# A halt in GpSimd's load queue, and a new order of the first two head pairs, in a fused attention and feed-forward kernel

## The chip, the cores and the metric

The kernel runs on one core of one Trainium2 chip. The metric is the device time of one execution in microseconds (us), as the median of the runs. TensorE is called PE in the profile (PEld for its weight loads), VectorE DVE, ScalarE ACT, GpSimd POOL and SyncE SP. A time in the trace counts from the start of the profiled span.

## What is computed

The reference is attention with a relative position bias, and behind it two matrix products with a leaky ReLU between them. Cut to what matters:

```python
B, H, S, D = 8, 8, 576, 64
scores = q @ k.T / sqrt(D) + bias_table[bucket(i - j)]   # per batch and head, 576 x 576
attn   = softmax(scores)
x      = (attn @ v)  # heads side by side: 4608 tokens x 512
h      = x @ w_in    # 512 x 2048
out    = max(0.01 * h, h) @ w_out                          # 2048 x 512
```

## The kernel before, in words

Work is tiled by head pairs: 8 batches of 4 pairs, 32 items, and n is the number of the item. A pair's q and k are turned on PE into `qt` and `kt` (`transpose_q`, `transpose_k`, lines 290 to 302); ACT copies q out of PSUM in the first pairs (line 293), DVE copies k (line 300) and masks its tail (`apart`, line 285). `kt` has two buffers, so the k of pair n overwrites that of pair n-2.

`score(n, u)` (line 823) makes one part of the scores on PE and their exponential on ACT. There are six parts: u = 0 to 3 give 128 keys each against 512 queries of both heads (PE line 322, ACT line 335, 128x1024), u = 4 the last 64 queries (PE line 315, ACT line 338 twice), u = 5 the last 64 keys (PE lines 325 and 326, ACT line 342). PSUM holds two score tiles for u = 0 to 3 and 5, so PE's third score waits for ACT to have read the first. Below, "s03" is short for score(0, 3), and so on.

The bias is applied after the exponential, as a product: `band(n, u)` (line 358, DVE) multiplies the part of the weights near the diagonal with a table `hk` (or `hk4` for the last 64 keys). The table is built at the start: ACT and DVE make one row of 512 numbers for each head, SP writes it to DRAM (line 189) and reads it back shifted for each partition (`load_hk`, `load_hk4`, lines 190 to 208) in the order: heads 0 and 1 of `hk`, pair 0 of `hk4` (two loads), heads 2 and 3 of `hk`, the other pairs of `hk4` (two loads), heads 4 to 7 of `hk`.

Then `av_tails(n)` and `av(n, e)` (PE lines 371 and 382) multiply the weights with v for the two heads, DVE divides (`divide`, lines 391 and 393), and `x_transposes` (PE line 443, DVE line 444) turns the pair's output into `xT`, from which the feed-forward pieces are made: `ffn_in` (PE line 469), `leaky` (ACT line 482 mostly), `ffn_out` (PE line 510).

All five engines have an order written out by hand (`manual_schedule`): each runs its instructions in the order of the calls. q, k, v and the weights are loaded, with a cast to bf16, by DMAs that GpSimd issues one after another. Each of GpSimd's loads also waits, by a semaphore that it shares, for the load eight before it. Their order at the start (lines 154 and 218 to 230, then `loads(0)`, line 782) is: q and k of heads 0 and 1; of 2 and 3; of 4 and 5; v of head 0; v of head 1; the two halves of the v tails of batch 0 (`load_v_tail`, line 130); v of head 2; v of head 3; q and k of heads 6 and 7; q and k of batch 1, heads 0 to 3; v of heads 4 to 7 in four parts (line 119); the ones columns of batch 1's v (two memsets); q and k of batch 1, heads 4 to 7; the first half of `w_in`; v of batch 1 in four parts and its tails; the second half of `w_in`; and `w_out`.

The first four pairs run in the loop of lines 832 to 870, with no feed-forward work beside them as no `xT` is complete. In it the order for n = 0 on PE is: s02, k of pair 1, three dummy matmuls (`spin(3)`, line 774), s03, q of pair 1, three dummy matmuls, s05, s04, s10, s11. For n = 1: the bands of pair 0 (DVE), k of pair 2, three dummy matmuls, s12, `av_tails(0)`, `av(0, 0)`, `band(1, 0)`, s13, q of pair 2, `av(0, 1)`, s15, `band(1, 1)`, s20, `x_transposes(0)`, `band(1, 2)`, s14, s21. From n = 4 on feed-forward pieces stand between the parts of a pair.

`tick` (line 780) is a tile of one element. GpSimd copies one element of an earlier pair's output into it (line 796) ahead of a group of later loads, so these are issued only after that pair.

Of the kernel before, what the change touches and what calls it, by code (L numbers as in the profile page):

```python
# [11 lines left out]
BF16 = mybir.dt.bfloat16  # L12
# [25 lines left out]
def kernel(  # L38
# [10 lines left out]
    nc = tc.nc  # L49

    B, H, S, D = q.shape
# [4 lines left out]
    P = 128  # L56
    n_pairs = H // 2
    NJ = S // P
    SL = S - NJ * P
# [10 lines left out]
    per = ctx.enter_context(tc.tile_pool(name="per", bufs=1))  # L70
# [20 lines left out]
    hk = per.tile([P, H, 3 * P], BF16, name="hk")  # L91
    hk4 = per.tile([P, n_pairs, P + SL], BF16, name="hk4")

    NBUF = 2
# [5 lines left out]
    v4 = [per.tile([P, n_pairs, D + 1], BF16, name=f"v4_{i}") for i in range(NBUF)]  # L100
# [8 lines left out]
    def load_qk(b, h0, h1):  # L109
        i = b % NBUF  # L110
        for src, dst in ((q, qn[i]), (k, kn[i])):
            nc.gpsimd.dma_start(  # L112
                out=dst[0:RQ, h0:h1, :, :].rearrange("r h c d -> r h (c d)"),
                in_=src[b, h0:h1, :, :].rearrange("h (r c) d -> r h (c d)", c=NC),
            )
# [8 lines left out]
    def load_v_head(b, h):  # L124
        nc.gpsimd.dma_start(  # L125
            out=vn[b % NBUF][:, :, h, 0:D],
            in_=v[b, h, 0 : NJ * P, :].rearrange("(c s) d -> s c d", s=P),
        )

    def load_v_tail(b):  # L130
        for e in range(2):
            nc.gpsimd.dma_start(
                out=v4[b % NBUF][e * SL : (e + 1) * SL, :, 0:D],
                in_=v[b, e::2, NJ * P : S, :].rearrange("h s d -> s h d"),
            )

    def clear_v(eng, i):
# [40 lines left out]
    for j, (u, lo, w, m) in enumerate(groups):  # L178
        copy = nc.scalar.copy if j % 3 == 2 else nc.vector.tensor_copy
        copy(out=ub[:, C0 + lo : C0 + lo + m * w].rearrange("h (m w) -> h m w", w=w),  # L180
             in_=e8[:, u : u + m].unsqueeze(2).to_broadcast([H, m, w]))
    row = ub[:, :]
    nc.vector.tensor_copy(
        out=ub[:, C0 - BAND + 1 : C0],
        in_=bass.AP(tensor=row.tensor, offset=row.offset + C0 + BAND - 1,
                    ap=[list(row.ap[0]), [-1, BAND - 1]]),
# [23 lines left out]
    def mirrored(t, lo, hi):  # L210
# [4 lines left out]
        ap[-1][0] = -1  # L215
        return bass.AP(tensor=v.tensor, offset=v.offset + hi - lo - 1, ap=ap)

    load_qk(0, 2, 4)
    load_qk(0, 4, 6)
    clear_edges(nc.vector, 1)  # L220
    load_v_head(0, 0)
    load_v_head(0, 1)
    load_v_tail(0)
    load_v_head(0, 2)
    load_v_head(0, 3)
    load_qk(0, 6, H)
# [39 lines left out]
    def turned_pair(n, j):  # L266

        if by_dma(n):
            return turned[n][:, j * NC : (j + 1) * NC, :].rearrange("p c r -> p r c")
        ps = ps_m_pool.tile([P, 8 * P], BF16, name="ps_t", tag="m")  # L270
        b, p = items[n]
        for c in range(NC):
            if n > n_pairs + 1:
                nc.tensor.transpose(ps[:, c * RQ : (c + 1) * RQ], in_=prs[n][:, j, c, :],
                                    identity=ident[0:RQ, 0:RQ])
                continue
            for e in range(2):
                nc.tensor.transpose(ps[e * D : (e + 1) * D, c * RQ : (c + 1) * RQ],
                                    in_=(qn, kn)[j][b % NBUF][0:RQ, 2 * p + e, c, :],
                                    identity=ident[0:RQ, 0:RQ])  # L280
        return ps[:, 0:S].rearrange("p (c r) -> p r c", c=NC)

    def apart(t):

        nc.vector.tensor_tensor(
            out=t[:, S : S + P].rearrange("p (e i) -> p e i", e=2),
            in0=t[:, NJ * P : S].unsqueeze(1).to_broadcast([P, 2, SL]),
            in1=own, op=ALU.mult)

    def transpose_q(n):  # L290
        qt = qts[n] = qt_pool.tile([P, S], BF16, name="qt")
        copy = nc.scalar.copy if n <= n_pairs else nc.vector.tensor_copy
        copy(out=qt[:, 0:S].rearrange("p (r c) -> p r c", c=NC), in_=turned_pair(n, 0))

    def transpose_k(n):
        kt = kts[n] = kts_[n % 2]
        t = turned_pair(n, 1)
        cuts = [0, -(-P // NC), RQ] if n == 0 else [0, RQ]
        for lo, hi in zip(cuts, cuts[1:]):
            nc.vector.tensor_copy(out=kt[:, lo * NC : hi * NC].rearrange("p (r c) -> p r c", c=NC),  # L300
                                  in_=t[:, lo:hi, :])
        apart(kt)
# [41 lines left out]
    def band(n, u):  # L344
        b, p = items[n]
        at, at4 = at_view(n), at4_[n % 2]
        hp = hk[:, 2 * p : 2 * p + 2, :]
        if u == 0:
            o, m = at[:, :, 0, 0 : 2 * P], mirrored(hp, P, 3 * P)
        elif u in (1, 2):  # L350
            o, m = at[:, :, u, (u - 1) * P : (u + 2) * P], mirrored(hp, 0, 3 * P)
        elif u == NJ:
            o, m = at[:, :, 3, 2 * P : S], mirrored(hp, 0, S - 2 * P)
        elif u == NJ + 1:
            o, m = at4[:, 3 * P : S], mirrored(hk4[:, p, :], 0, P + SL)
        else:
            return
        nc.vector.tensor_tensor(out=o, in0=o, in1=m, op=ALU.mult)  # L358
# [3 lines left out]
    def av_tails(n):  # L362

        b, p = items[n]
        at4 = at4_[n % 2]
        ops_[n] = op_pool.tile([P, NJ + 1, 2 * D], BF16, name="opair")
        ps = outs[n] = [ps_o_pool.tile([P, 512], FP32, name="ps_o", tag=f"o{e}") for e in range(2)]
        for ic in range(NJ + 1):
            for e in range(2):
                r = slice(e * SL, (e + 1) * SL)  # L370
                nc.tensor.matmul(ps[e][:, ic * (D + 1) : (ic + 1) * (D + 1)],  # L371
                                 lhsT=at4[r, ic * P : (ic + 1) * P], rhs=v4[b % NBUF][r, p, :],
                                 start=(ic == 0), stop=False)

    def av(n, e):
        b, p = items[n]
        at = at_[n % 2]
        ps = outs[n][e][:, 0 : (NJ + 1) * (D + 1)].rearrange("p (i d) -> p i d", d=D + 1)
        for ic in range(NJ + 1):
            for c in range(NJ):  # L380
                o = (e * NJ + c) * S + ic * P
                nc.tensor.matmul(ps[:, ic, :], lhsT=at[:, o : o + P], rhs=vn[b % NBUF][:, c, 2 * p + e, :],  # L382
                                 start=False, stop=(ic == NJ and c == NJ - 1))
        divide(n, (e,))
# [40 lines left out]
    def x_by_dma(n):  # L425
        return n_pairs + 2 <= n < N - 1 and n != 2 * n_pairs - 1

    def x_transposes(n, spare=None):
        b, p = items[n]
        opair = ops_[n]  # L430
        w = (NJ + 1) * P
        if x_by_dma(n):
            nc.sync.dma_start_transpose(
                out=xT[p][:, b * S : b * S + w].rearrange("p (i t) -> p i t", t=P),
                in_=opair.rearrange("p i d -> p (i d)"),
            )
            return
        if spare is None:
            ps = ps_m_pool.tile([P, 8 * P], BF16, name="ps_tx", tag="m")
        else:  # L440
            ps = ps_o_pool.tile([P, 8 * P], BF16, name="ps_tx", tag=spare)
        for ic in range(NJ + 1):
            nc.tensor.transpose(ps[:, ic * P : (ic + 1) * P], in_=opair[:, ic, :], identity=ident)  # L443
        nc.vector.tensor_copy(out=xT[p][:, b * S : (b + 1) * S], in_=ps[:, 0:S])
# [326 lines left out]
    def spin(k):  # L771
        pw = ps_o_pool.tile([P, 512], FP32, name="ps_w", tag="o0")
        for _ in range(k):
            nc.tensor.matmul(pw, lhsT=ones[:, 0:P], rhs=ones, start=True, stop=True)
# [2 lines left out]
        for u in range(NJ + 2):  # L777
            band(n, u)

    tick = per.tile([1, 1], BF16, name="tick")  # L780

    def loads(n, behind_pair=2):

        b, p = items[n]
# [22 lines left out]
    def begin(n):  # L807
        loads(n)
        if by_dma(n + 1):
            turn_ahead(n)  # L810
# [12 lines left out]
    def score(n, u):  # L823
        exp(n, u, qk_mm(n, u))
# [4 lines left out]
    spin(2)  # L829
    score(0, 0)  # L830
    score(0, 1)
    for n in range(n_pairs):
        begin(n)
        if n > 1:
            band(n - 1, 5)
            band(n - 1, 4)
        if n == 1:
            for u in (0, 1, 2, 5, 4):
                band(0, u)
        if n == 0:  # L840
            score(n, 2)
        transpose_k(n + 1)
        if n < 2:
            spin(3)
        if n > 0:
            score(n, 2)
            av_tails(n - 1)
            av(n - 1, 0)
            band(n, 0)
        score(n, 3)  # L850
        if n == 1:
            transpose_q(n + 1)
        if n > 0:
            av(n - 1, 1)
        if n != 1:
            transpose_q(n + 1)
        if n < 1:
            spin(3)
        score(n, 5)
        if n > 0:  # L860
            band(n, 1)
        if n == 1:
            score(n + 1, 0)
        if n > 0:
            x_transposes(n - 1)
            band(n, 2)
        score(n, 4)
        if n != 1:
            score(n + 1, 0)
        score(n + 1, 1)  # L870

    n = n_pairs
# [141 lines left out]
```

## Time and profile before

| | before |
|---|---|
| median of 3 runs | 370.7 us |
| range of the runs | 370.27 to 371.1 us |
| profiled execution, its own time | 370.79 us |
| profiled execution, its span | 369.0 us |
| PE busy in the span | 360.6 us (98%) |
| ACT busy in the span | 245.7 us (67%) |
| DVE busy in the span | 192.9 us (52%) |

The span reaches from the first to the last instruction of the program; the 1.8 us between it and the execution's own time lie around it. A timeline row gives the start, the time to the end of the last instruction of the row, the engine, line, operation and operands, how many instructions are merged, and in brackets the idle time of the engine before the row and what ended it. DMA queue q0 is that of the loads that GpSimd issues, q1 that of SP's.

### The profile page before, as it was taken

Reading aid. Unit: us, or ns where it says so; the run is one execution under the profiler, and the core shown is the slowest. Engines: PE = TensorE matmul, PEld = TensorE weight load, DVE = VectorE, ACT = ScalarE, POOL = GpSimd, SP = SyncE. Lnnn points to the kernel's source line nnn. Section 1 sums busy time; section 2 is a strip of 40 time slices with the busy share of each in tenths; the row PEclk is TensorE's granted clock in tenths of the full one; section 3 lists DMA queues with packets and bytes.
Section 4 is the critical chain, followed back from the end, with each engine's and each line's share of the span. In section 5 each row is a group of like instructions: output and inputs, shape, how many; then the busy total and the mean of one; then the engine's idle time right before and its main releaser. Section 6 shows DMA issues by size and latency. Waiting matters only on the chain.

```text
span 369.0 us, 10548 instructions
## 1 busy us (share of the span) xinstructions
PE 360.6 (98%) x4496; PEld 188.1 (51%) x4496; DVE 192.9 (52%) x502; ACT 245.7 (67%) x382; POOL 75.4 (20%) x118
## 2 busy tenths in 40 slices
PE   7989999999999999999999999999999999999996
PEld 2555555555555555555555545455555544444443
DVE  4688687776757576766765556665554200200000
ACT  5998887479847797777877777777777365055111
POOL 8853431063006300630053006100000000000000
PEclk9999999999999999999999999999999999999999
DMA  8999999969937992899099558933111000110212
GB/s 107 191 197 183 206 203 141 160 114 154 136 80 126 172 155 53 120 157 197 20 134 183 115 80 97 174 98 72 28 47 50 28 30 0 69 47 0 76 69 85
DMA packets 104358, 40.17 MB, mean 109 GB/s; under 512 B 83184, under 2 KB 98808, under 8 KB 104312
## 3 DMA queue, kind: packets, MB, share of 16 engines
q0 software_dynamic: 53696, 18.36, 49.3%
q1 hardware_dynamic: 49320, 19.06, 29.2%
q10 hardware_dynamic: 1296, 2.10, 1.6%
q8 instruction: 35, 0.57, 0.6%
q14 instruction: 11, 0.09, 0.1%
HBM read 37.68 MB, written 9.45 MB: 128 GB/s over the span
## 4 chain that ended last, share of the span: by engine, by line
PE 91%; DMA 4%; POOL 2%; DVE 1%; ACT 1%; issue 1%; ACTq 0%; POOLq 0%
PE pm L469 30%; PE pm L510 28%; PE pm L629 9%; PE ps_s L322 7%; PE ps_o L417 6%; DMA vn<-in_v_dram 4%; PE ps_o L382 4%; PE ps_s L325 2%; PE ps_o L371 1%; PE ps_q L315 1%; PE pm L503 1%; PE ps_tx L443 1%; POOL vn L125 1%; POOL kn L112 1%; POOL qn L112 0%
## 5 line engine op out<-in xcount | busy, mean ns | idle before, releaser
L335 ACT ACTIVATE at<-ps_s 128x1024 bf16<-128x1024 f32 x128 | 124.8, 1026 | 25.2 <-PE ps_s L322 24.9
L482 ACT ACTIVATE gt<-pm 128x512 bf16<-128x512 f32 x138 | 83.2, 603 | 69.4 <-PE pm L469 68.8
L469 PE MATMUL pm<-xT,w_in_sb 128*128 128x512 bf16 x508 | 117.2, 379 | 0.1
L510 PE MATMUL pm<-w_out_sb,gt 128*128 128x512 bf16 x476 | 110.5, 380 | 0.0
L358 DVE TENSOR_TENSOR at<-at,hk 128x768 bf16<-128x768 bf16 (+3 forms) x160 | 70.7, 453 | 55.5 <-ACT at L335 31.3
L469 PEld LDWEIGHTS <-w_in_sb 128*128 128x128 bf16 x508 | 47.9, 98 | 55.2
L510 PEld LDWEIGHTS <-gt 128*128 128x128 bf16 x476 | 43.4, 98 | 49.6
L322 PE MATMUL ps_s<-qt,kt 64*128 64x512 bf16 x256 | 43.4, 380 | 2.2 <-ACT at L335 1.6
L629 PE MATMUL pm<-w_out_sb,gt 64*128 64x512 bf16 x168 | 42.0, 376 | 0.0
L523 DVE COPY y<-pm 128x512 f32<-128x512 f32 x28 | 19.4, 691 | 41.4 <-PE pm L510 41.4
L629 PE MATMUL pm<-xT,w_in_sb 64*128 64x512 bf16 x136 | 37.5, 376 | 0.0
L393 DVE TENSOR_TENSOR opair<-ps_o,rcp 128x320 bf16<-128x320 f32 x64 | 29.7, 488 | 1.4
L796 POOL COPY tick<-opair 1x1 bf16<-1x1 bf16 x18 | 3.2, 180 | 130.7 <-DVE opair L393 130.7
L119 POOL DMA_DIRECT2D vn<-in_v_dram x32 | 28.0, 887 | 8.8 <-DMA w_out_sb<-in_moe_w_out_dram 4.6
L417 PE MATMUL ps_o<-vn,at 64*128 64x65 bf16 x1520 | 29.5, 190 | 0.0
L417 PEld LDWEIGHTS <-at 64*128 64x128 bf16 x1520 | 27.1, 94 | 4.4 <-SPq L401 3.0
L322 PEld LDWEIGHTS <-kt 64*128 64x128 bf16 x256 | 11.5, 94 | 22.5 <-issue 13.3
L342 ACT ACTIVATE at<-ps_s 128x576 bf16<-128x576 f32 x32 | 21.8, 682 | 0.2 <-PE ps_s L326 0.2
L338 ACT ACTIVATE at<-ps_q 128x256 bf16<-128x256 f32 x64 | 21.3, 395 | 0.4 <-PE ps_q L315 0.3
L391 DVE RECIPROCAL rcp<-ps_o 128x5 f32<-128x5 f32 x64 | 10.0, 181 | 21.1 <-PE ps_o L382 18.0
L382 PE MATMUL ps_o<-vn,at 128*128 128x65 bf16 x520 | 20.4, 194 | 0.1
L382 PEld LDWEIGHTS <-at 128*128 128x128 bf16 x520 | 17.9, 97 | 3.3 <-issue 0.9
(65 smaller groups left out, 257.4 us busy)
## 6 DMA issues: line engine op xcount, KB each, us to landing
out_dram<-y SPq DMA_DIRECT2D x28, 256.0 KB, 2.5
qn<-in_q_dram POOLq DMA_DIRECT2D x14, 288.0 KB, 7.3
kn<-in_k_dram POOLq DMA_DIRECT2D x14, 288.0 KB, 9.2
vn<-in_v_dram POOLq DMA_DIRECT2D x28, 128.0 KB, 9.7
w_in_sb<-in_moe_w_in_dram POOLq DMA_DIRECT2D x2, 1024.0 KB, 12.9
w_out_sb<-in_moe_w_out_dram POOLq DMA_DIRECT2D x2, 1024.0 KB, 15.9
out_dram<-y ACTq DMA_DIRECT2D x7, 256.0 KB, 2.0
qn<-in_q_dram POOLq DMA_DIRECT2D x4, 144.0 KB, 3.8
```

The source lines that it names most:

```text
L119: nc.gpsimd.dma_start(out=vn[b % NBUF][:, c, h0:h1, 0:D], in_=v[b, h0:h1, c * P : (c + 1) * P, :].rearrange("h s d -> s h d"),)
L322: nc.tensor.matmul(ps[:, e, :], lhsT=kt[r, u * P : (u + 1) * P], rhs=qt[r, 0:512], start=True, stop=True)
L335: nc.scalar.activation(at[:, :, u, 0:512], ps, AF.Exp, scale=scale)
L342: nc.scalar.activation(at4[:, 0:S], ps.rearrange("p e i -> p (e i)")[:, 0:S], AF.Exp, scale=scale)
L358: nc.vector.tensor_tensor(out=o, in0=o, in1=m, op=ALU.mult)
L382: nc.tensor.matmul(ps[:, ic, :], lhsT=at[:, o : o + P], rhs=vn[b % NBUF][:, c, 2 * p + e, :], start=False, stop=(ic == NJ and c == NJ - 1))
L393: nc.vector.tensor_tensor(out=opair[:, :, e * D : (e + 1) * D], in0=ps[:, :, 0:D], in1=rcp.to_broadcast([P, NJ + 1, D]), op=ALU.mult)
L417: m = nc.tensor.matmul(outs[n][e][:, ic * (D + 1) : (ic + 1) * (D + 1)], lhsT=at[halves[r], o : o + P], rhs=vn[b % NBUF][halves[r], c, 2 * ...
L469: nc.tensor.matmul(pm, lhsT=w_in_sb[:, c, f * P : (f + 1) * P], rhs=xT[c][:, t0 : t0 + TT], start=(c == 0), stop=(c == n_cc - 1))
L482: nc.scalar.activation(g, pm, AF.Prelu, bias=0.0, scale=1.0, alpha=0.01)
L510: nc.tensor.matmul(pm, lhsT=gt[:, f, ts * P : (ts + 1) * P], rhs=w_out_sb[:, f, :], start=(f == 0), stop=(f == n_fc - 1))
L629: m = nc.tensor.matmul(pm, lhsT=w[halves[r]], rhs=x[halves[r]], start=(k == 0 and c == 0), stop=(low is not None and k == 1 and c == n_cc ...
```

## The change

The change does four things. `load_v_tail` takes a range of pairs. At the start, the v tails of pair 0 are loaded as before, behind v of heads 0 and 1; then GpSimd copies one element of `hk` (partition 0, head 0) into `tick`, for which it has to wait until the load of heads 0 and 1 of `hk` has landed; only then it issues the v tails of pairs 1 to 3 (two loads more than before in all) and all that follows. The loop over the first four pairs is written out for n = 0 and n = 1: s03 now comes straight behind s02, ahead of k and q of pair 1; the transposes of pair 2's k come straight behind s04, ahead of s10, which also puts DVE's copy and mask of that k ahead of the bands of pair 0; one of the three groups of three dummy matmuls is gone, one stands between q of pair 1 and s05, one between s11 and s12. For n = 2 and 3 the order is that of before.

```diff
-    def load_v_tail(b):
+    def load_v_tail(b, p0=0, p1=n_pairs):
         for e in range(2):
             nc.gpsimd.dma_start(
-                out=v4[b % NBUF][e * SL : (e + 1) * SL, :, 0:D],
-                in_=v[b, e::2, NJ * P : S, :].rearrange("h s d -> s h d"),
+                out=v4[b % NBUF][e * SL : (e + 1) * SL, p0:p1, 0:D],
+                in_=v[b, 2 * p0 + e : 2 * p1 : 2, NJ * P : S, :].rearrange("h s d -> s h d"),
             )
...
+    tick = per.tile([1, 1], BF16, name="tick")
     load_qk(0, 2, 4)
     load_qk(0, 4, 6)
     clear_edges(nc.vector, 1)
     load_v_head(0, 0)
     load_v_head(0, 1)
-    load_v_tail(0)
+    load_v_tail(0, 0, 1)
+    nc.gpsimd.tensor_copy(out=tick, in_=hk[0:1, 0, 0:1])
+    load_v_tail(0, 1)
     load_v_head(0, 2)
     load_v_head(0, 3)
     load_qk(0, 6, H)
...
-    for n in range(n_pairs):
+    begin(0)
+    score(0, 2)
+    score(0, 3)
+    transpose_k(1)
+    transpose_q(1)
+    spin(3)
+    score(0, 5)
+    score(0, 4)
+    transpose_k(2)
+    score(1, 0)
+    score(1, 1)
+
+    begin(1)
+    for u in (0, 1, 2, 5, 4):
+        band(0, u)
+    spin(3)
+    score(1, 2)
+    av_tails(0)
+    av(0, 0)
+    band(1, 0)
+    score(1, 3)
+    transpose_q(2)
+    av(0, 1)
+    score(1, 5)
+    band(1, 1)
+    score(2, 0)
+    x_transposes(0)
+    band(1, 2)
+    score(1, 4)
+    score(2, 1)
+
+    for n in range(2, n_pairs):
         begin(n)
...
```

More of the change, by code (lines that the diff above doesn't have):

```diff
@@ L778, in bands @@
             band(n, u)
-    tick = per.tile([1, 1], BF16, name="tick")
     def loads(n, behind_pair=2):
@@ L831 @@
     score(0, 1)
[L832 to L866 removed]
+    begin(0)
[28 more added lines that the diff above has]
+    for n in range(2, n_pairs):
+        begin(n)
+        band(n - 1, 5)
+        band(n - 1, 4)
+        transpose_k(n + 1)
+        score(n, 2)
+        av_tails(n - 1)
+        av(n - 1, 0)
+        band(n, 0)
+        score(n, 3)
+        av(n - 1, 1)
+        transpose_q(n + 1)
+        score(n, 5)
+        band(n, 1)
+        x_transposes(n - 1)
+        band(n, 2)
         score(n, 4)
[L868 to L869 removed]
+        score(n + 1, 0)
         score(n + 1, 1)
```

## Prediction

> **What bounds the kernel now.** I read the table of stretches first, then the timelines of ACT, DVE, PE and GpSimd up to 34 us (only the start is changed), and last the chain of waits.
>
> ```profile
> core 0: us, PE busy (x) PEld busy (x) DVE busy (x) ACT busy (x) POOL busy (x), PEclk, DMA share, GB/s
> 6.78:33.31 26.53, 23.23 (x418) 14.38 (x419) 18.89 (x50) 25.58 (x36) 17.39 (x26) 1.00 1.51 188
> ```
> ```profile
> 33.31:360.00 326.69, 326.21 (x4000) 168.32 (x4000) 170.87 (x429) 215.99 (x336) 52.42 (x80) 1.00 0.77 104
> ```
>
> The columns are the stretch, its length, then each engine's busy time. From the first exponential at 6.78 to 33.31 it is ACT that is full: 25.58 of 26.53 us. From there to 360 it is PE: 326.21 of 326.69. The change touches the first stretch alone. What it wins or loses there is passed on whole, since PE behind it has no room to catch up and no room to gain. ACT's work is the same in both kernels, so no more than 26.53 - 25.58 = 0.95 us can be won, 0.26% of the time. There is no such bound on the side of a loss.
>
> ```profile
> 6.78 3.99 ACT L335 ACTIVATE at<-ps_s 128x1024 bf16<-128x1024 f32 x4 [1.22 <-PE ps_s L322]
> 10.66 0.63 ACT L293 COPY qt<-ps_t 128x576 bf16<-128x576 bf16 x1
> 11.18 0.67 ACT L342 ACTIVATE at<-ps_s 128x576 bf16<-128x576 f32 x1
> 11.72 0.68 ACT L338 ACTIVATE at<-ps_q 128x256 bf16<-128x256 f32 x2
> 12.25 4.04 ACT L335 ACTIVATE at<-ps_s 128x1024 bf16<-128x1024 f32 x4
> ...
> 18.75 2.88 ACT L335 ACTIVATE at<-ps_s 128x1024 bf16<-128x1024 f32 x3
> ...
> 23.05 0.66 ACT L338 ACTIVATE at<-ps_q 128x256 bf16<-128x256 f32 x2 [0.33 <-PE ps_q L315]
> ```
> ```profile
> L335 ACT ACTIVATE at<-ps_s 128x1024 bf16<-128x1024 f32 x20 | 19.4, 1047 | 1.6 <-PE ps_s L322 1.2
> ```
>
> The last row groups the large exponentials of this stage: one takes 1047 ns, but they overlap. Where nothing stops ACT (the row of three at 18.75) one starts each (2.88 - 1.05) / 2 = 0.92 us. Four should take 3 x 0.92 + 1.05 = 3.81; the first two rows of four are 0.2 us longer, as PE brought the fourth scores late. The longest gap is 0.33 us at 23.05.
>
> ```profile
> 15.61 9.88 DMA vn<-in_v_dram
> 25.49 0.04 issue
> 25.53 0.69 PE ps_o L382 x17
> ```
>
> The chain of waits, in order of time, says what else holds this stage: the last part of v of heads 4 to 7 lands at 25.49, and PE, in the middle of `av(2, 0)`, goes on at 25.53. So a load sets the pace there, and PE and ACT are dense behind it.
>
> **The fourth scores sooner.**
>
> ```profile
> 9.31 0.39 PE L322 MATMUL ps_s<-qt,kt 64*128 64x512 bf16 x2
> 9.63 0.45 PE L278 MATMUL ps_t<-ident,qn 96*64 96x96 bf16 x12
> 10.01 0.83 PE L774 MATMUL ps_w<-const-bfloat16-1.0 128*128 128x512 bf16 x3
> 10.67 0.38 PE L325 MATMUL ps_s<-qt,kt 128*128 128x512 bf16 x1
> 10.89 0.19 PE L326 MATMUL ps_s<-qt,kt 128*128 128x64 bf16 x1
> 11.01 0.29 PE L315 MATMUL ps_q<-qt,kt 64*128 64x64 bf16 x8
> ```
>
> s03 now waits only for its PSUM tile, that is for the end of the second exponential, 6.78 + 0.92 + 1.05 = 8.75; it starts at about 8.8 instead of 9.31. ACT starts the fourth exponential at 6.78 + 3 x 0.92 = 9.54 instead of 6.78 + 3.99 - 1.05 = 9.72, 0.2 us sooner. Behind s03, from start to start by these rows: k of pair 1 +0.32, q +0.38, dummies +0.38, s05 +0.66 = 10.54, its end 0.41 later at 10.95. ACT wants it at 9.54 + 0.92 + 0.52 = 10.98, so it just holds, and s10's exponential comes at 12.05 instead of 12.25.
>
> **The third pair's k sooner, and the bands.**
>
> ```profile
> 8.66 0.76 DVE L300 COPY kt<-ps_t 128x576 bf16<-128x576 bf16 x1 [1.67 <-PE ps_t L278]
> 9.45 0.22 DVE L285 TENSOR_TENSOR kt<-kt,own 128x128 bf16<-128x128 bf16 x1
> 12.37 1.93 DVE L358 TENSOR_TENSOR at<-at,hk 128x512 bf16<-128x512 bf16 x5 [2.69 <-DMA hk<-u_row]
> ...
> 21.17 0.42 DVE L358 TENSOR_TENSOR at<-at,hk 128x512 bf16<-128x512 bf16 x1 [0.20 <-DMA hk<-u_row]
> ```
>
> Before, DVE waits 2.69 us for the table. In the new order pair 2's k stands ahead of the bands: s04 starts at 10.54 + 0.34 = 10.88, the transposes 0.12 to 0.29 behind it, they take 0.45, DVE's copy and mask 0.97 (0.76 + 0.22, nearly end to end). So the bands of pair 0 can't start before 12.4 to 12.6, however soon the table lands, against 12.37 before. `av(0, 0)` waits for them and s13 stands behind it on PE, so s13 stays where it was, and the 0.2 us that ACT won is waited off in front of it. The two moves together: 0 to +0.2 us, I take +0.05, by the earlier start of the transposes. What DVE gains behind the bands (the copy no longer stands there) is hidden: its next work waits for `av(0, 0)` anyway.
>
> **Dummy matmuls.** Three fewer free 0.66 us of PE where PE waits for bands or ACT: nothing. That PE then runs slower would need a lower granted clock.
>
> ```profile
> 24.00:26.00 2.00, 1.21 (x31) 0.96 (x31) 1.16 (x3) 2.00 (x3) 2.00 (x3) 1.00 1.29 205
> ```
>
> At 24 to 26 us PE is busy only 1.21 of 2.00 us and the clock stays at 1.00. The emptier places of the new order (0.5 us ahead of s03, 0.45 ahead of s12) are shorter. Cost 0, bounded by those places.
>
> **The halt.**
>
> ```profile
> 7.23 1.27 POOL L132 DMA_DIRECT2D v<-in_v_dram  x2
> ...
> 10.56 0.71 POOL L112 DMA_DIRECT2D kn<-in_k_dram  x1
> ```
> ```profile
> 7.75 0.41 SPq L191 DMA_DIRECT2D hk<-u_row  x1
> ```
> ```profile
> L796 POOL COPY tick<-opair 1x1 bf16<-1x1 bf16 x18 | 3.2, 180 | 130.7 <-DVE opair L393 130.7
> ```
>
> Queued behind `tick` on GpSimd are the other v tails, v of heads 2 and 3, q and k of heads 6 and 7, and all that follows. When does it end? SP issues the table's first part at 7.75, and DVE's wait for it ended at 12.37. Its landing, from the rows of three of GpSimd's loads (the first q load, with nothing ahead; k of heads 4 and 5; k of heads 6 and 7):
>
> ```profile
> DMA to landing us min/median/max: 3.1/3.1/3.1
> ```
> ```profile
> DMA to landing us min/median/max: 4.4/4.4/4.4
> ```
> ```profile
> DMA to landing us min/median/max: 6.5/6.5/6.5
> ```
>
> Without v of heads 2 and 3 beside it, the table's part can't land sooner than the load with nothing ahead (7.75 + 3.1 = 10.9) nor later than before (12.37); I take 11.4, since v of heads 0 and 1 is still ahead of it. With 0.18 for the copy GpSimd goes on at 11.6 (11.1 to 12.6). From the first tail to k of heads 6 and 7 it needed 10.56 - 7.23 = 3.33 us, for the same kinds of loads: that k is issued at 14.9 (14.4 to 15.9) instead of 10.56. Before it landed at 10.56 + 6.5 = 17.1, in time for its transposes (18.02, below). With the queue emptied by the halt it takes 3.1 to 4.4 us: 17.5 to 20.3. I take 3.6, nearer to the emptied one: 18.5. [...]
>
> The transposes of pair 3's k and s23, before:
>
> ```profile
> 18.02 0.45 PE L278 MATMUL ps_t<-ident,kn 96*64 96x96 bf16 x12
> ...
> 19.88 0.39 PE L322 MATMUL ps_s<-qt,kt 64*128 64x512 bf16 x2
> ```
>
> PE then waits about 0.45 us at these transposes. Of this 0.3 is free: s23 starts 1.86 behind them and ends at 20.27, while ACT takes it at 18.75 + 2.88 - 1.05 = 20.6. Against the rest stands a gain: the table's last load (heads 4 to 7) is no longer held up, and DVE's 0.20 us wait at 21.17 goes, which is part of what makes ACT's gap of 0.33 at 23.05. Net 0 to +0.1 us for a landing at 18.5; 1 us more for each us beyond.
>
> **The last part of v.**
>
> In the first fence the DMA share of the stretch is 1.51 and the rate 188 GB/s: the engines are always busy, and GpSimd's loads and the table's compete for them. The table is 128 x (8 x 384 + 4 x 192) numbers of two bytes, 0.98 MB; at 188 GB/s that is 5.2 us of traffic, all of it due before 25.49 in both kernels. So the halt, some 3 us long, is filled by it: the same bytes in another order, and the last part of v again lands at 25.5. Term 0. It sits behind all of the above: up to 0.1 us of lateness at 25 us is hidden in it, and anything won ahead of it is lost in it. The first half of `w_in` is loaded behind it and moves with it.
>
> **Sum.** +0.05 + 0.05 + 0 = +0.1 us. The profiled execution took 370.79 us (span 369.0 and 1.8 around it): 370.9. The median of the runs, 370.7, is 0.1 lower, so 370.8 us. A measurement of this kernel tells about 0.2% (0.74 us) from no change.
>
> **The rivals.**
>
> 1. Slower: k of heads 6 and 7 is late. It decides from 18.5; at 19.5 the loss is 1.0 + 0.1, 371.8 us, at 20.3 it is 372.6. For it: six issues of 0.6 to 0.8 us now stand between the table's landing and this load, with less than 1 us of slack before. Against: the queue is empty when it starts. Chance 0.20.
> 2. Slower: the DMA engines run dry. From the table's landing to the first resumed bytes pass 0.2 us and about half of 3.1; if the table's other loads don't fill that, up to 1.8 us of traffic is lost, the last part of v lands by so much later: 371.5 to 372.6. Against: the table's 0.98 MB. Chance 0.10.
> 3. Faster: with the table out of the way early, the last v part lands sooner than 25.49, and the gaps of ACT from 15 us on go. From 0.33 to most of 0.95 us: 370.2. [...] Against: no byte is saved. Chance 0.15, a third of it below 369.96.
> 4. The halt brings nothing: the table lands at 12.37 as before, held up by something else than GpSimd's loads. k is then issued at 15.9, lands at 19.0 or later (3.1): 0.2 us from later bands and 0.5 from k, 371.5. Chance 0.10.
>
> My forecast has the remaining 0.45, with 370.5 to 371.2 as its own range.
>
> **How the numbers follow.** Faster by over 0.2% needs nearly all of ACT's idle time: 0.06. Slower by over 0.2% (over 371.44) takes most of rival 1, two thirds of rival 2, half of rival 4: 0.28. Within: 0.66. The range leaves out the far ends of rivals 1 and 2 and the third of rival 3: 370.1 to 372.1.
>
> **What would show it.** ACT's first row of four at 3.8 us, and a gap of about 0.4 us ahead of s13; bands from about 12.4 with a release by DVE's own work, not by the table; GpSimd going on at 11.1 to 12.6; PE waiting at pair 3's k until about 18.5; the last part of v at 25.5. It would be wrong if the bands start well ahead of 12.4, or if one of these two loads lands 0.7 us or more off.

## The result and the profile after

| | before | after |
|---|---|---|
| median of 10 runs each, side by side | 370.75 us | 374.26 us |
| range of the runs | 370.27 to 372.24 us | 371.43 to 375.43 us |
| ratio after / before, 95% interval | | 1.0078 [1.0049, 1.0107] |
| profiled execution, its own time (span) | 370.79 us (369.0) | 375.43 us (373.7) |
| last part of v of heads 4 to 7 lands | 25.49 us | 28.27 us |
| first feed-forward piece on PE | 33.24 us | 37.91 us |

The change makes the kernel 3.5 us slower by the medians, and 2.9 us by the means, whose ratio the table gives; 370.8 us with a range up to 372.1 was predicted. The profiled execution of after is the slowest of its ten runs, so its trace shows the loss at its largest: the first feed-forward piece comes 4.67 us later, and the execution takes 4.64 us longer. In after all line numbers of the compute steps are three higher than in before (PE's scores are L325 for L322, the exponential L338 for L335, the bands L361 for L358, `av` L385 for L382, the feed-forward piece L472 for L469); in e4 below they are ten higher than in before.

The table of stretches of after, cut at its first feed-forward piece:

```profile
core 0: us, PE busy (x) PEld busy (x) DVE busy (x) ACT busy (x) POOL busy (x), PEclk, DMA share, GB/s
6.78:37.98 31.20, 24.81 (x417) 15.86 (x416) 19.34 (x51) 25.96 (x37) 19.38 (x30) 0.89 1.43 170
37.98:364.00 326.02, 325.54 (x3997) 168.23 (x3997) 171.14 (x429) 215.70 (x336) 51.80 (x78) 1.00 0.79 103
```

Behind 37.98 nothing has changed: 326 us, filled by PE, as from 33.31 on before. All of the loss lies in the start, where ACT does the same 26 us of work but now in 31.20 us, and where two columns have fallen: the granted clock of PE from 1.00 to 0.89, and the DMA rate from 188 to 170 GB/s. The chain of waits of after says through what the start ends late:

```profile
7.82 4.32 DMA hk<-u_row
12.14 0.05 issue
12.19 0.18 POOL tick L225
12.37 0.06 issue
12.43 1.24 POOL v L132 x2
...
17.82 2.19 POOL vn L119 x3
20.00 8.27 DMA vn<-in_v_dram
28.27 0.04 issue
28.31 1.09 PE ps_o L385 x17
...
37.91 1.04 PE pm L472 x4
```

The path now leads from the table's first part over the halt and GpSimd's issues into the last part of v. That part is issued at 20.00 (before: 15.61) and lands at 28.27 (before: 25.49). Behind its landing stand 9.60 us up to the first feed-forward piece; before, 25.53 to 33.24, there were 7.71. So the 4.67 us are 2.78 us of a later landing, and 1.89 us by which the work behind it has become slower. PE's timeline and the table by 2 us around the landing show the second part:

```profile
19.29 0.45 PE L281 MATMUL ps_t<-ident,kn 96*64 96x96 bf16 x12 [1.15 <-DMA kn<-in_k_dram]
...
25.14 0.45 PE L281 MATMUL ps_t<-ident,kn 96*64 96x96 bf16 x12 [1.07 <-DMA kn<-in_k_dram]
...
26.55 0.19 PE L385 MATMUL ps_o<-vn,at 128*128 128x65 bf16 x1 [0.36 <-DMA vn<-in_v_dram]
27.75 0.19 PE L385 MATMUL ps_o<-vn,at 128*128 128x65 bf16 x1 [1.01 <-DMA vn<-in_v_dram]
28.31 1.09 PE L385 MATMUL ps_o<-vn,at 128*128 128x65 bf16 x17 [0.37 <-DMA vn<-in_v_dram]
```

```profile
26.00:28.00 2.00, 0.58 (x7) 0.29 (x4) 0.61 (x2) 0.97 (x2) 2.00 (x3) 0.97 1.35 196
28.00:30.00 2.00, 1.69 (x22) 1.16 (x22) 0.52 (x2) 0.01 (x1) 2.00 (x4) 0.50 1.14 211
30.00:32.00 2.00, 2.00 (x33) 1.63 (x33) 1.26 (x5) 1.13 (x2) 1.16 (x2) 0.50 1.13 212
32.00:34.00 2.00, 2.00 (x20) 1.21 (x19) 1.44 (x4) 1.79 (x5) 0.00 (x0) 0.50 1.85 176
34.00:36.00 2.00, 2.00 (x48) 1.58 (x45) 1.13 (x4) 2.00 (x3) 0.45 (x1) 0.82 2.49 156
```

From 24 us on PE waits for k of pair 4 and then piece by piece for v. In 26 to 28 us it is busy 0.58 of 2.00 us, and then the clock falls to 0.50. It stays there until 34.7: in 34 to 36 it is 0.82 on average, that is 0.72 us at half speed. All of PE's matmuls in between take longer (the last row of PE's timeline, 17 of `av` in 1.09 us, against 17 in 0.69 us on the chain of before), and PE, not ACT, is full.

The DMA rates, before and then after, in stretches of 6 to 8 us (last column GB/s):

```profile
6.00:14.00 8.00, 6.96 (x80) 2.94 (x79) 3.57 (x10) 7.11 (x10) 8.00 (x12) 1.00 1.40 167
14.00:20.00 6.00, 5.61 (x123) 3.98 (x123) 5.45 (x14) 5.88 (x10) 3.16 (x8) 1.00 1.25 219
20.00:26.00 6.00, 4.41 (x96) 2.96 (x95) 4.77 (x14) 5.67 (x9) 4.16 (x5) 1.00 1.62 189
```

```profile
6.00:14.00 8.00, 6.13 (x74) 2.61 (x72) 4.48 (x12) 7.17 (x11) 4.07 (x8) 1.00 1.11 178
14.00:20.00 6.00, 4.54 (x99) 3.11 (x101) 4.32 (x12) 5.52 (x9) 6.00 (x9) 1.00 1.16 133
20.00:26.00 6.00, 4.83 (x110) 3.15 (x104) 4.78 (x13) 5.61 (x9) 3.35 (x8) 1.00 1.62 163
```

In total bytes nothing is lost during the halt itself: the table's loads fill it, and up to 14 us after has even moved (178 - 167) x 8 us = 0.09 MB more. The hole comes behind it. From 14 to 20 us before moves 219 GB/s, after 133: 86 x 6 us = 0.52 MB less. The net 0.43 MB at the 163 GB/s of the next stretch are 2.6 us, nearly the 2.78 by which v is late. In before the table's later loads and a long line of GpSimd's loads run side by side in this stretch; in after the table is nearly through, and GpSimd's loads begin again with small ones, one issue each 0.6 to 0.8 us. The two queues from 14 to 20 us, before and then after (packets, MB, and the time that the packets took as a share of 16 engines):

```profile
q0 software_dynamic: 1209, 0.78, 86.8%
q1 hardware_dynamic: 899, 0.52, 36.8%
```

```profile
q0 software_dynamic: 2064, 0.61, 104.7%
q1 hardware_dynamic: 267, 0.19, 11.6%
```

Most of the drop in this stretch, 0.33 of 0.5 MB, is table (q1) that after had moved before 14 us, 0.80 MB against 0.46. GpSimd's queue (q0) is 0.27 MB behind at 14 us (0.60 against 0.87) and 0.44 MB behind at 20: the halt opens the gap, and the restart, with more but smaller packets, widens it instead of closing it. Whether this reading holds is what the experiments ask.

### The profile page after: what moved, and what is told of

The parts are those of the page before. It is cut to its first block, busy times and chain, and to the rows that moved or that the text cites. A ratio compares the mean times of both kernels' runs of the same rounds, so it can differ in the third digit from the quotient of the medians.

```text
span 373.7 us, 10544 instructions
## 1 busy us (share of the span) xinstructions
PE 362.4 (97%) x4493; PEld 189.8 (51%) x4493; DVE 193.6 (52%) x502; ACT 246.1 (66%) x382; POOL 76.8 (21%) x121
## 4 chain that ended last, share of the span: by engine, by line
PE 91%; DMA 5%; POOL 2%; ACT 1%; DVE 1%; issue 0%; ACTq 0%; DVEq 0%
PE pm L472 30%; PE pm L513 28%; PE pm L632 9%; PE ps_s L325 8%; PE ps_o L420 6%; PE ps_o L385 4%; DMA vn<-in_v_dram 2%; PE ps_s L328 2%; PE ps_o L374 1%; DMA hk<-u_row 1%; PE ps_q L318 1%; DMA u_row<-ub 1%; PE pm L506 1%; PE ps_tx L446 1%; POOL vn L119 1%; DMA tabT<-in_bias_table_dram 1%
## 5 line engine op out<-in xcount | busy, mean ns | idle before, releaser
L338 ACT ACTIVATE at<-ps_s 128x1024 bf16<-128x1024 f32 x128 | 125.1, 1026 | 28.5 <-PE ps_s L325 28.5
L472 PE MATMUL pm<-xT,w_in_sb 128*128 128x512 bf16 x508 | 117.2, 379 | 0.1
L361 DVE TENSOR_TENSOR at<-at,hk 128x768 bf16<-128x768 bf16 (+3 forms) x160 | 70.8, 453 | 52.7 <-ACT at L338 31.3
L472 PEld LDWEIGHTS <-w_in_sb 128*128 128x128 bf16 x508 | 48.1, 98 | 55.1
L325 PE MATMUL ps_s<-qt,kt 64*128 64x512 bf16 x256 | 44.0, 385 | 1.9 <-ACT at L338 1.5
L119 POOL DMA_DIRECT2D vn<-in_v_dram x32 | 27.9, 883 | 6.8 <-PE pm L472 4.3
L385 PE MATMUL ps_o<-vn,at 128*128 128x65 bf16 x520 | 21.8, 198 | 1.7 <-DMA vn<-in_v_dram 1.7
L325 PEld LDWEIGHTS <-kt 64*128 64x128 bf16 x256 | 11.6, 94 | 22.0 <-issue 12.9
L385 PEld LDWEIGHTS <-at 128*128 128x128 bf16 x520 | 19.0, 100 | 5.4 <-issue 2.9
```

The source lines that it names most:

```text
L119: nc.gpsimd.dma_start(out=vn[b % NBUF][:, c, h0:h1, 0:D], in_=v[b, h0:h1, c * P : (c + 1) * P, :].rearrange("h s d -> s h d"),)
L325: nc.tensor.matmul(ps[:, e, :], lhsT=kt[r, u * P : (u + 1) * P], rhs=qt[r, 0:512], start=True, stop=True)
L338: nc.scalar.activation(at[:, :, u, 0:512], ps, AF.Exp, scale=scale)
L472: nc.tensor.matmul(pm, lhsT=w_in_sb[:, c, f * P : (f + 1) * P], rhs=xT[c][:, t0 : t0 + TT], start=(c == 0), stop=(c == n_cc - 1))
```

## The experiments

Theory A: the halt is the whole cause. GpSimd's queue runs empty, starts again alone and with small loads, and so the last part of v is late; the new order on PE costs nothing. Theory B: the new order or the missing dummies cost the time, by PE's gaps or by its clock. Within A it is open how much the slow clock adds to the late load, and whether the halt hurts by standing still or by the empty queue behind it. The landing and the first feed-forward piece in the table are those of each kernel's profiled execution; "halted" is GpSimd's idle time ahead of `tick`.

| kernel | halted | last v lands | first piece | profiled | median | ratio to before, 95% interval |
|---|---|---|---|---|---|---|
| e1, no halt | none | 25.1 | 32.9 | 370.39 | 371.37 | 1.0004 [0.9989, 1.0019] |
| e2, halt only | 3.92 | 28.1 | 37.6 | 375.17 | 374.78 | 1.0074 [1.0043, 1.0106] |
| e3, 12 dummies at `av` | 3.44 | 26.6 | 36.1 | 373.65 | 373.99 | 1.0090 [1.0059, 1.0120] |
| e4, v ahead of q | 3.81 | 24.7 | 34.1 | 371.99 | 372.55 | 1.0031 [1.0018, 1.0044] |
| e5, late halt | 0.27 | 26.7 | 34.4 | 371.93 | 370.66 | 0.9985 [0.9973, 0.9998] |
| e6, whole tails | 4.06 | 27.9 | 36.8 | 374.33 | 372.67 | 1.0046 [1.0021, 1.0072] |
| e7, no halt, v ahead | none | 23.7 | 33.0 | 370.92 | 370.44 | 0.9968 [0.9951, 0.9986] |
| e8, 6 dummies at `av` | 3.24 | 26.7 | 36.7 | 374.25 | 373.68 | 1.0066 [1.0047, 1.0085] |
| e9, longer halt | 5.19 | 28.2 | 36.0 | 373.55 | 374.02 | 1.0088 [1.0072, 1.0105] |
| e10, dummies in three places | 3.61 | 27.8 | 35.6 | 373.12 | 373.42 | 1.0066 [1.0050, 1.0083] |
| e11, before with v ahead | none | 23.5 | 35.9 | 373.46 | 370.68 | 0.9999 [0.9984, 1.0014] |
| e12, late halt, v ahead | 0 | 23.7 | 33.0 | 370.74 | 370.63 | 0.9987 [0.9970, 1.0003] |

The medians of before beside them were 371.18 us (e1 to e4), 371.26 (e5 to e8) and 370.98 (e9 to e12).

**e1: the change without the halt.**

```diff
-    nc.gpsimd.tensor_copy(out=tick, in_=hk[0:1, 0, 0:1])
```

> The changed kernel without the copy into tick: GpSimd's loads go on at once, the four v-tail loads and the new order of the first two pairs stay. Theory A (the halt makes the loads late): the last part of v of heads 4 to 7 lands at 25.2 to 25.8 us as before, PE's granted clock stays at 1.00, the time is 370.5 to 371.2 us. Theory B (the new order of the first two pairs, with three dummy matmuls fewer, costs the time): 373 to 375 us, with the clock at 0.5 for some us around 30.

It keeps the new order, the fewer dummies and the two more loads. It took 371.37 us, 0.2 above before's median and above the 370.5 to 371.2 of theory A, but within the interval of no change. One stretch of its table:

```profile
14.00:20.00 6.00, 5.25 (x120) 3.76 (x121) 4.65 (x13) 5.67 (x10) 4.11 (x8) 1.00 1.26 216
```

The DMA rate of before (219) is back, and v lands at 25.1. The new order with its fewer dummies and its two more loads costs nothing that can be measured.

**e2: the kernel before with the halt alone.**

```diff
-    load_v_tail(0)
+    load_v_tail(0, 0, 1)
+    nc.gpsimd.tensor_copy(out=tick, in_=hk[0:1, 0, 0:1])
+    load_v_tail(0, 1)
```

> The kernel before with the split v tails and the halt alone; the order of the pairs and all dummy matmuls as before. Theory A (the halt): the last part of v at 27.5 to 28.5 us, 373 to 375 us, and 371.5 to 372.5 in executions where the clock stays up. Theory B (the order): 370.5 to 371.2 us.

374.78 us: the whole loss, with the old order on PE and all its dummies. The two of its eight runs in which the clock stayed up took 372.28 and 372.37, as expected. Two stretches:

```profile
14.00:20.00 6.00, 4.35 (x95) 2.93 (x93) 4.93 (x14) 5.53 (x9) 6.00 (x9) 1.00 1.22 147
...
28.00:30.00 2.00, 1.91 (x26) 1.38 (x26) 0.74 (x3) 0.23 (x1) 2.00 (x4) 0.50 1.15 212
```

The rate falls to 147 GB/s, and the clock to 0.50 behind the same wait for v. With e1 this settles that the halt, and not the order or the dummies, makes the loss; B falls.

**e3: twelve dummy matmuls ahead of the wait for v.**

```diff
         score(n, 2)
+        if n == 3:
+            spin(12)
         av_tails(n - 1)
```

> The changed kernel with 12 dummy matmuls (2.6 us) ahead of av_tails(2), where PE waits for v. If the slow clock is a loss of its own: the last part of v still lands at 28.3, the clock stays at 1.00, the first feed-forward piece starts at about 36 instead of 37.9, the time is 372.0 to 373.0 us and spreads less. If the clock only follows the wait and costs nothing beside it: 374 to 375 us.

In the profiled execution the clock held and the first piece came at 36.1, as expected; two of the six runs still had a mean clock of 0.995. The median of 373.99 is above the 372 to 373 that I gave. In its trace the dummies outlast the load:

```profile
25.17 2.80 PE L777 MATMUL ps_w<-const-bfloat16-1.0 128*128 128x512 bf16 x12
28.02 0.33 PE L374 MATMUL ps_o<-v,at 64*128 64x65 bf16 x10
```

v landed at 26.6 in this execution, not at 28.3 as I had expected, and PE was free at 27.97. So this run doesn't price the clock; it trades one loss for another.

**e8: half as many dummies.**

```diff
+        if n == 3:
+            spin(6)
```

> The changed kernel with 6 dummy matmuls (1.3 us) ahead of av_tails(2), which end before v is there. If they suffice to hold the clock: 1.00 throughout, first feed-forward piece at 35.5 to 36.5, 372.0 to 373.2 us, under the 374.0 us with 12, of which some came after v had landed. If they don't: the clock at 0.5 around 30 us, 374 to 375 us.

373.68 us. In its profiled execution the clock fell in another place:

```profile
18.00:20.00 2.00, 0.68 (x14) 0.50 (x12) 1.35 (x4) 1.87 (x4) 2.00 (x3) 0.87 1.03 128
20.00:22.00 2.00, 2.00 (x38) 1.53 (x32) 0.98 (x2) 1.02 (x1) 1.63 (x5) 0.50 1.29 167
```

At 18 to 20 us PE waits for pair 3's k (1.32 us here), is busy 0.68 of 2.00 us, and loses the clock there. The halt opens three gaps, and dummies in one of them leave the others.

**e10: dummies in all three gaps.**

```diff
         band(n - 1, 4)
+        spin(4)
         transpose_k(n + 1)
         score(n, 2)
+        if n == 3:
+            spin(4)
         av_tails(n - 1)
```

> The changed kernel with four dummy matmuls ahead of the turning of pair 3's k, four ahead of that of pair 4's k and four ahead of the last tail weights, that is in each of the three places where PE waits. If the clock's drops are a separate part of the loss on top of the late loads, no run has a mean granted clock under 0.999, and the median is that of the changed kernel's own runs at full clock, 371.4 to 372.4, plus up to 0.5 for dummies that outlast a wait: 372.0 to 373.0, lowest and highest less than 2 us apart. If the loss is the late loads alone, 373.7 to 374.3 as with the dummies in one place.

The mean granted clock was 0.999 or 1.000 in each of the six runs, and they lie within 1.7 us. The median was 373.42 us, 0.4 above the range that I gave for the clock as a separate part and 0.3 below the range for the late loads alone. Against before it is 2.44 us, where the change itself lost 3.51. Its trace shows no drop of the clock, v at 27.8 (2.3 us later than before) and the first piece at 35.60 (2.4 us later). So with the clock held the lateness of v is passed on about one to one. By the medians some 2.4 of the change's 3.5 us would then be the late loads and about 1 the clock; by the ratios of the means, 1.0066 and 1.0078, the clock's part is under half a us. The intervals, [1.0050, 1.0083] and [1.0049, 1.0107], overlap widely, so this split is rough.

**e4: the changed kernel with v ahead of q.**

```diff
-    load_qk(1, 0, H // 2)
+    load_one(1, 0, H // 2, k, kn)
     load_v_part(0, range(NJ), 4, H)
+    load_one(1, 0, H // 2, q, qn)
```

`load_one` makes the load of q alone or of k alone out of `load_qk`.

> The changed kernel, halt included, with the loads of batch 1 and of v in another order: k of batch 1 (heads 0 to 3), v of heads 4 to 7, and only then q of batch 1. If what costs the time is that v of heads 4 to 7 and k of pair 4 land late: they land 2 us or more sooner (25 to 26 and 21 to 23 us), the clock stays up, 371 to 372 us. If the time is lost anywhere else (pair 3's k, the bands, the order): 373 us or more.

372.55 us, somewhat above the 371 to 372 that I expected. v lands at 24.7, sooner than before the change, although the halt stands (3.81 us) and the rate from 14 to 20 us is as low as in e2:

```profile
14.00:20.00 6.00, 4.09 (x89) 2.84 (x89) 4.06 (x11) 5.48 (x9) 6.00 (x9) 1.00 1.24 147
```

```profile
19.70 0.45 PE L288 MATMUL ps_t<-ident,kn 96*64 96x96 bf16 x12 [1.60 <-DMA kn<-in_k_dram]
...
34.12 1.04 PE L479 MATMUL pm<-xT,w_in_sb 128*128 128x512 bf16 x4 [0.28 <-DVE kt L295]
```

So it is v's place in the line that costs most. The clock stayed up in this trace, but five of the twelve runs had 0.995. With v early, the wait for pair 3's k, in the shadow of v otherwise, becomes what is left: 1.60 us on PE, a first piece 0.88 us later than before, and 1.4 us in the median.

**e5: the halt behind q and k of heads 6 and 7.**

```diff
-    nc.gpsimd.tensor_copy(out=tick, in_=hk[0:1, 0, 0:1])
     load_v_tail(0, 1)
     load_v_head(0, 2)
     load_v_head(0, 3)
     load_qk(0, 6, H)
+    nc.gpsimd.tensor_copy(out=tick, in_=hk[0:1, 0, 0:1])
```

> The changed kernel with the halt six loads later: the copy into tick stands behind q and k of heads 6 and 7, so six loads are queued while GpSimd waits for the table. Theory A1 (the loss comes from GpSimd's queue running empty): GpSimd still waits about 1 us, but no traffic is lost; the last part of v lands at 25 to 26 us, the time is 370.6 to 371.6 us. Theory A2 (every us that GpSimd stands still is lost, full queue or not): the last part of v about 1 us later than before, 26 to 27 us, 371.8 to 372.8 us.

```profile
12.62 0.18 POOL L229 COPY tick<-hk 1x1 bf16<-1x1 bf16 x1 [0.27 <-DMA hk<-u_row]
```

```profile
14.00:20.00 6.00, 4.55 (x95) 3.06 (x97) 4.50 (x14) 5.37 (x9) 4.37 (x9) 1.00 1.22 211
```

GpSimd waits for the same load until about the same time, 12.62 against 12.19, but has issued six more loads by then; the rate is 211 GB/s and the median 370.66 us, not slower than before. So the wait does no harm in this place. Theory A2 isn't refuted by it: GpSimd stood still for only 0.27 us here, not the 1 us that I had expected, so a long wait with loads still under way was not tested. And in the profiled execution, at 371.93 us the slowest of the twelve, v landed at 26.7, in the range that I had given for A2.

**e6: the halt where it was, with all v tails in two loads ahead of it.**

```diff
-    load_v_tail(0, 0, 1)
+    load_v_tail(0)
     nc.gpsimd.tensor_copy(out=tick, in_=hk[0:1, 0, 0:1])
-    load_v_tail(0, 1)
```

> The changed kernel with the v tails of all pairs in their two loads ahead of the halt, so two short issues of 0.6 us fewer stand behind it (48 KB of 128-byte rows). If GpSimd's issuing is the bound behind the halt (64 KB or less for each 0.6 to 0.8 us of issue): k of heads 6 and 7 and the last part of v land 1.0 to 1.3 us sooner than with the change (18.0 and about 27), 372.5 to 373.5 us. If the transfer itself is the bound: 0.3 us sooner at most, 373.8 to 375 us. In both the table lands at 12.1 to 12.6, not later by more than 0.3.

372.67 us: two issues fewer behind the halt are worth 1.6 us against the changed kernel's median (2.1, if each is taken against before beside it), though the halt is as long (4.06 us). q of heads 6 and 7 is issued 1.7 us after GpSimd goes on (14.27 against 12.55) instead of 3.0 (15.18 against 12.19). The median lies in the range for issuing as the bound. The landings don't: in the profiled execution, of 374.33 us, k of heads 6 and 7 landed at 19.0 and v at 27.9, 0.3 and 0.4 us sooner than in after, where 18.0 and about 27 were expected and 0.3 at most if the transfer is the bound. The last part of v was issued 0.9 us sooner (19.08 against 20.00), and less than half of that came through. The intervals [1.0021, 1.0072] and [1.0049, 1.0107] overlap as well. How much of the loss is the small issues behind the halt stays open.

**e9: a longer halt.**

```diff
-    nc.gpsimd.tensor_copy(out=tick, in_=hk[0:1, 0, 0:1])
+    nc.gpsimd.tensor_copy(out=tick, in_=hk[0:1, 2, 0:1])
```

> GpSimd waits for the second part of the table's heads (2 and 3) instead of the first: it goes on at about 13.2 us instead of 12.4. Theory A (the loss is the time in which GpSimd's queue is empty, passed on to the last part of v): pair 3's k and the last v part land about 0.8 us later than with the halt as it was, first feed-forward piece at 38.5 or later in a run whose clock drops, median 0.5 to 1.2 us above the changed kernel's (374.8 to 375.5). Theory B (a halt of any length disturbs the order of the bytes, and the loss is the same): 374.3. Theory C (only the dropped clock counts): 374.3 too, as the clock drops already.

```profile
13.53 0.27 POOL L225 COPY tick<-hk 1x1 bf16<-1x1 bf16 x1 [5.19 <-DMA hk<-u_row]
```

```profile
20.64 0.45 PE L281 MATMUL ps_t<-ident,kn 96*64 96x96 bf16 x12 [2.53 <-DMA kn<-in_k_dram]
```

GpSimd goes on 1.3 us later than in the changed kernel, and pair 3's k comes 1.4 us later (20.6 against 19.2). But v landed at 28.2, as with the shorter halt, and the median was 374.02 us, below the 374.8 to 375.5 of theory A and near the 374.3 of B and C. So "each us of halt is a us of v" is not borne out. In this trace the clock was low from 22.3 to 25.7 us, ahead of v's landing, and the chain to the first feed-forward piece (35.98) runs through pair 3's k and not through v. One reason for v can be seen: landings scatter. The executions with the same halt (after, e2, e3, e8, e10) show v at 28.3, 28.1, 26.6, 26.7 and 27.8 us, for a GpSimd that went on within 11.6 to 12.3. Why the longer halt did not add to v's landing stays open.

**e7, e11 and e12: without an early halt, and v ahead of q.** e7 is e1 with the three lines of e4, e11 is the kernel before with them, e12 is e5 with them.

> The new order of the first two pairs without the halt, and with v of heads 4 to 7 loaded ahead of q of batch 1 (k of batch 1 first). If the landing of v at 25.5 us still held the kernel before by some tenths: the last part of v at 23 to 24 us, 370.2 to 370.8 us, 0.1 to 0.3 us under the kernel before beside it. If ACT alone holds it: no difference, within 0.2 us.

> The kernel before, with only the order of loads changed: k of batch 1, v of heads 4 to 7, q of batch 1. If the gain of the version without halt (370.4) comes from the load order alone, 370.2 to 370.7; if it needs the new order of the first pairs too, about as before, 370.9 to 371.3.

> The new order of the first pairs, the halt behind the loads of q and k of heads 6 and 7, and the loads in the order k of batch 1, v of heads 4 to 7, q of batch 1. With seven loads still on their way at the halt it costs nothing, so about as the version without halt: 370.1 to 370.6, and at most 0.3 us better, since the table's last parts meet fewer of GpSimd's loads.

e7 took 370.44 us in the median, 0.82 below before beside it where 0.1 to 0.3 was expected, ratio 0.9968 [0.9951, 0.9986], and all its twelve runs lie within 0.9 us (370.02 to 370.92), where before's 29 spread over 3.4. It is faster than before by 0.3%, and not only by the clock: the 22 of before's runs that kept theirs have a median of 371.16. Its v lands at 23.7, 1.8 us ahead of before's 25.49, with 207 GB/s from 14 to 20 us:

```profile
14.00:20.00 6.00, 4.98 (x111) 3.49 (x112) 4.64 (x14) 5.19 (x8) 4.39 (x9) 1.00 1.35 207
```

e11, with the order of loads alone, has a median of 370.68 us, at the upper end of the range that I gave for the load order as the whole gain, but a ratio of 0.9999 [0.9984, 1.0014]; e12, with the late halt, has 0.9987 [0.9970, 1.0003]. The intervals of the three overlap, so whether the new order of the first pairs is needed for the gain is not settled. The profiled execution of e11, at 373.46 us the slowest of its twelve, lost its clock early (0.70 on average from 6 to 14 us), which fits its late first piece in the table.

## Why the prediction was wrong, point by point

**Held: where the loss is passed on.** Nothing behind the start gave any of it back: 4.67 us at the first piece, 4.64 in the profiled execution.

**Held: the fourth scores and the bands.** ACT's timeline of after:

```profile
6.83 3.77 ACT L338 ACTIVATE at<-ps_s 128x1024 bf16<-128x1024 f32 x4 [1.16 <-PE ps_s L325]
...
12.05 2.95 ACT L338 ACTIVATE at<-ps_s 128x1024 bf16<-128x1024 f32 x3
15.32 1.02 ACT L338 ACTIVATE at<-ps_s 128x1024 bf16<-128x1024 f32 x1 [0.32 <-PE ps_s L325]
```

The first four exponentials take 3.77 us (3.81 said), s10's comes at 12.05 (said), and the 0.2 us won are waited off ahead of s13 at 15.32 (a gap of 0.32; 0.4 said). DVE's timeline:

```profile
12.28 0.23 DVE L288 TENSOR_TENSOR kt<-kt,own 128x128 bf16<-128x128 bf16 x1
12.43 1.93 DVE L361 TENSOR_TENSOR at<-at,hk 128x512 bf16<-128x512 bf16 x5
```

The bands start at 12.43, directly behind DVE's own work, as said (12.4 to 12.6). e1 prices both moves together with the dummies: 371.37 us beside 371.18, against the +0.05 that the sum gave them.

**Within its bounds, at the late end: the table and k.** The table's first part landed at 12.14 and GpSimd's next load was issued at 12.43 (11.1 to 12.6 given, 11.6 taken). The halt bought hardly anything here: without it (e1) this part landed at 12.3, as in before, so in these executions the premise of the fourth rival, that the halt does not bring the table sooner, came true. k of heads 6 and 7 landed at 19.2 (17.5 to 20.3 given, 18.5 taken), and PE waited 1.15 us for it. By the prediction's own rule, 0.1 at 18.5 and 1 us more for each us beyond, this alone is 0.8 us, the first rival. In e4, where it is what is left, k landed at 19.7: 1.3 by the rule, 0.88 at the first piece and 1.4 in the median.

**Failed: "Term 0", the last part of v.** The step was that the DMA engines "are always busy", so that "the halt, some 3 us long, is filled by" the table, "the same bytes in another order, and the last part of v again lands at 25.5". The first half is right, the rates up to 14 us show it. But I reckoned the bytes at one rate, the mean of 188 GB/s, whatever runs beside what. The rate was not one number: from 14 to 20 us it was 219 GB/s with both queues at work (216 in e1, 211 in e5) and 133 to 147 once the table had been moved ahead and GpSimd's line had begun again with small loads (after, e2, e4). That GpSimd's loads run alone is not by itself the reason, as 28 to 30 us of after, alone too, has 211 GB/s. So the same bytes took 2.8 us longer. The prediction had the sign of it in its own working: it moved the issue of k of heads 6 and 7 from 10.56 to 14.9 with the line, but left the last part of v, further back in the same line, where it was. Its issue moved by 4.4 us (15.61 to 20.00).

The second rival had the place right (engines run dry behind the table's landing) and gave it 0.10 and at most 1.8 us; it looked for the hole in the time until the first resumed bytes. That time the table does fill (208 GB/s from 12 to 14 us); the hole is behind it, 94 GB/s from 15 to 17 us, when the small loads follow one by one. How much of that is issue time and how much the transfer of small packets is not separated. From 20 to 22 us of before GpSimd's queue alone moved 1920 packets, 0.33 MB, mostly small ones too, against 1196 packets and 0.17 MB from 15 to 17 us of after, so small packets alone don't set the lower rate; e6 speaks against issue time as the whole of it.

That the stretch from 14 to 20 us moves 216 GB/s in e1 and 147 in e2 is in good part a matter of when: 0.22 of the 0.41 MB between them is table that e2 had moved before 14 us.

**Failed with it: "Cost 0, bounded by those places", the clock.** I looked for gaps on PE only where the edits of PE's order make some. The late loads make the gaps: in after PE is busy 0.85 of 2.00 us at 18 to 20 us, 0.93 at 24 to 26 and 0.58 at 26 to 28. Of after's ten runs two had a mean granted clock of 1.000 (371.43 and 372.30 us), five 0.995 (372.62 to 374.97) and three 0.990 or 0.991 (375.08 to 375.43). These groups do not price the clock, since the loads may come at other times in them too, which the runs without a trace do not show; e10 prices it roughly, at half a us to 1 us. The traces give a second price, from single executions whose chain runs through v. From v's landing to the first feed-forward piece they take 7.75 us where the clock holds (before, and e5), 8.89 with 3.4 us of half speed behind the landing (e6), and 9.58 and 9.64 with 6.8 us of it, nearly all behind the landing (e2 and after).

**The forecast** was thus right in each step on ACT, DVE and the order on PE, and wrong in the step that was argued from a mean rate, on the queue that the change stops, and in PE's clock, which hung on it.

## What to carry to other kernels

Before you stop a queue that feeds the bound stage, list what it carries up to the next load with a due time, in order, with the issue time of each, and reckon that line from the moment it starts again: an empty queue that restarts with small loads has its whole line still to go, and here it didn't catch up (0.27 MB behind before at 14 us, 0.44 at 20). Move the wait behind the loads that are due first (e5), or the load that is due first ahead in the line (e4), rather than argue that the bytes are the same. e4 won back only part, as k of pair 3, which stands ahead of v, was still late. And where a load may come late in front of PE, count the clock: in after, 3.41 us in which PE was busy for 1.38 were followed by 6.8 us at 0.50.

## What the runs showed of the hardware

- **The drops of the clock in the start of these traces lasted 3.4 or 6.8 us.** In after it was at 0.50 from 27.9 us (0.97 on average in 26 to 28, so 0.12 us of it) to 34.7, 6.8 us; in e2 it was 6.8 us too, in e6, e8 and e9 3.4 us. Over all runs of all kernels the mean clock is 0.999 to 1.000, 0.994 to 0.995, or 0.990 to 0.991. On a span of 373.7 us, 3.4 us at half speed take 3.4 / 2 / 373.7 = 0.0046 off the mean, so by this estimate a run lost none, one or two such pieces.
- **In the six traces with a drop in the start, PE was busy 1.35 to 2.00 of the 3.41 us ahead of it** (e6 1.35, after 1.38, e2 1.41, e9 1.63, e8 1.80, e11 2.00). The 3.41 us are the stretches of the clock's own record: from its first value, at 4.00 us, after has 23.89 us at 1.00, 6.83 at 0.50 and 337.92 at 1.00, that is 7, 2 and 99 times 3.41, and before has 365.23 us at 1.00 from 3.49 us on, 107 times. Of the other pieces of this length in the start the lowest were 2.59 us in before, 2.26 in after and 2.03 in e4, and the clock stayed. Two of the pieces, after's with a drop behind it and e4's without:

```profile
24.48:27.89 3.41, 1.38 (x27) 0.92 (x28) 1.26 (x3) 2.50 (x3) 2.25 (x3) 1.00 1.55 186
15.77:19.18 3.41, 2.03 (x38) 1.17 (x34) 2.74 (x8) 3.41 (x7) 3.41 (x6) 1.00 1.20 125
```

The clock came back after one piece where PE was busy all through it (e6, e8, e9), and only after the second where PE had stopped in the first (3.04 us busy in after, 3.03 in e2, 3.35 in e11). As the pieces start at other times in each execution (3.49 us in before, 4.00 in after), other gaps of PE fall into one piece. Busy time alone does not explain the drops: near the program's end the clock fell in after behind a piece with 1.37 us, and in e2, e8 and e9 it did not behind 1.46 to 1.74 us (their mean clocks are 0.991, 0.995 and 0.995, which the drops in the start account for). No run was made to find out what sets them.

- **The table's first part landed little sooner with the other queue stopped.** With GpSimd halted it took 4.32 us from its issue at 7.82, and landed at 12.14; in e1, where GpSimd went on, it took 4.3 from 8.02, and landed at 12.3. Over all traces it is 3.7 to 4.5 us with the early halt (eight traces, 4.0 in the middle; e8 3.75, e6 4.50) and 4.2 to 4.6 without (six, 4.35 in the middle; e7 4.63), so the halt brought some 0.3 us, within the scatter.
- **Even the kernel before loses the clock now and then**: 5 of the 26 runs beside e1 to e4 had 0.995 or less, and took 371.89 to 374.68 us. e7, whose v comes 1.8 us sooner, never did in twelve.
